# Spreading the routing of the last batch's two halves over the first chunk of expert 0

## The chip, the cores and the metric

The kernel runs on one core of one Trainium2 chip. The metric is the device time of one execution in microseconds (us). The kernel before was timed three times: 938.08, 938.54 and 939.94 us, median 938.54 us.

## The reference

Attention over 32 memory slots per head (4 batches, 8 heads, 576 tokens, head size 64) gives 2304 tokens of width 512. They go through a dense layer pair (512 to 2048, leaky ReLU, back to 512), and then through a mixture of 8 experts with the two best experts per token:

```python
logits = x @ w_gate
noisy_logits = logits + np.log1p(np.exp(x @ w_noise)) * noise
top2 = np.argpartition(-noisy_logits, 2, axis=1)[:, :2]
...
for e in range(E):
    for k in range(2):
        mask = top2[:, k] == e
        h = np.maximum(x[mask] @ w1[e], 0.0)
        out[mask] += top2_w[mask, k, None] * (h @ w2[e])
```

## The kernel before

**Numbers as pairs.** Matrices are held as a high and a low part (`w2h`/`w2l`, `gh`/`gl`, `xh`/`xl`), and a product is three matmuls. ScalarE (ACT) writes the high part by a copy, VectorE (DVE) the low part by a subtraction.

**The dense layers** run in 128 slots `n`. A slot is one batch `b` (0 to 3), one half `u` of its tokens (288 tokens) and one 128-wide piece `f` of the hidden layer. `l1(n)` computes the piece (L587, with L593, L598, L603, L608 behind it), and `l2(n - 2)` multiplies an earlier piece into four output banks (L625); after each fourth piece VectorE adds the banks to the result `big` (L628). Slots 120 to 127 are the last batch (b = 3): four pieces for half 0, four for half 1.

**The routing** of a half is the generator `post(b, u)`: gate logits (`pg` L650, `pl` L656, `lg` L658), the tokens transposed (`px` L665) and written to DRAM as `x2` (L667), the two best experts (L687 to L698), the place of each token in its expert's list by a count (`pr` L702 and L704, then small VectorE operations on `pos`, `blk`, `ri`), matrices of tokens against places (`xr`, L736 to L760), and six matmuls (`pi` L764) that VectorE adds into the lists `acc` (L766). It yields between its parts and runs as a `Job` of ten steps.

**What sets the order.** A job has a start `t0` and a due time `t1` in slots. `tick(t)`, called several times per slot, steps each job that is behind the straight line from `t0` to `t1`:

```python
def behind(self, t):
    return self.did < self.total * (t - self.t0) / max(self.t1 - self.t0, 0.5)
...
tick(len(slots) + 2 + (n + j / 3) * 1.4)   # in expert 0, first chunk, step n
```

A scheduler then places the instructions in each engine's queue. Each queue is worked off in order.

**Expert 0** is done in two chunks: 360 places that hold only tokens of the batches 0 to 2, and 256 places with the rest. For the first chunk the job `early` computes three columns of `get` and `put` (`places`, L770 to L772), gathers three tiles of rows from `x2` (`fetch`, L820, a GpSimd (POOL) indirect DMA into `row`) and transposes them (`turn`: `pxt` L833, `xh` L835, `xl` L836). A chunk has eight pieces of the hidden layer, each 12 matmuls in (`e1`, L858, then `gh` L861 and `gl` L862) and 9 out (`e2`, L876). After the last routing, `handover` computes the other places and fetches the second chunk's two tiles; their `turn` comes when the first chunk ends.

**Expert weights** are loaded by SyncE (SP) in pairs of pieces into two buffers each (`r1` L790, `r2` L792), and split by ScalarE (`w2h` L807) and VectorE (`w2l` L808). A load waits until VectorE has split what was in its buffer. Each call of the generator `weights` splits the two tiles of one piece.

Of the kernel before, what the change touches and what calls it, by code (L numbers as in the profile page):

```python
# [20 lines left out]
def moe_kernel(  # L21
# [18 lines left out]
    B, H, S, D = q.shape  # L40
# [16 lines left out]
    TP = 2  # L57
# [69 lines left out]
    def tick(t):  # L127
        used = 0
        for g in sorted(jobs, key=lambda g: (g.cost >= 0, g.t1)):
            while g in jobs and g.behind(t):  # L130
                if abs(g.cost) + held(g) + used > 2:
                    break
                used += max(g.cost, 0)
                g.step()
# [479 lines left out]
    def l2_db(n, db, eng=None):  # L614
        b, u, f = slots[n]
        first, last = f % 4 == 0, f % 4 == 3
        if first:
            YT[b, u, db] = psum.tile([128, TU], F32, name="py", tag="y", bufs=4)
        ghi, glo, _ = G[n]
        wh, wl = WO[f]  # L620
        py = YT[b, u, db]
        y = Y[:, 2 * b + u]
        s = slice(db * 128, db * 128 + 128)
        for i, (w_, g_) in enumerate(((wh, ghi), (wh, glo), (wl, ghi))):
            nc.tensor.matmul(py, w_[:, s], g_, start=(first and i == 0), stop=(last and i == 2))  # L625
        if last:
            if f > 3:
                nc.vector.tensor_add(y[:, db], y[:, db], py)  # L628
            elif eng is not None:
                eng.tensor_copy(y[:, db], py)  # L630
            else:
                nc.scalar.activation(y[:, db], py, AF.Copy)

    def l2(n):
        b, u, f = slots[n]
        for db in range(NDB):
            l2_db(n, db)
            if db == 1:
                tick(n + 2.5)
        if f == F1 // 128 - 1:  # L640
            Job(post(b, u), 10, n + 2, n + 2 + TP, 1)

    def post(b, u):
        def sm(shape, nm, dt=F32, bufs=2):
            return pp.tile([P] + shape, dt, name=nm, bufs=bufs)
# [55 lines left out]
        for j in range(HJ):  # L701
            nc.tensor.matmul(pr[:P, (j + 1) * E:(HJ + 1) * E], onesb, hit[:, j, None, :].to_broadcast([P, HJ - j, E]),  # L702
                             start=(j == 0), stop=False, skip_group_check=True)
        nc.tensor.matmul(pr[:P, :HJ * E], ups, hit.rearrange("p j e -> p (j e)"), start=False, stop=True,  # L704
                         skip_group_check=True)
        rk = sm([HJ, E], "rk")
        if (b, u) == (B - 1, 0):
            nc.vector.tensor_scalar(cnt[:, 0:1], cnt[:, 0:1], float(CB), None, op0=OP.max)
# [392 lines left out]
    for n in range(8, len(slots) + 2):  # L1101
        if n < len(slots):
            b, u, f = slots[n]
# [42 lines left out]
        if n >= 10:  # L1146
            f2 = slots[n - 2][2]
            while f2 not in WO:
                JW["o", f2 // 4].step()
            l2(n - 2)  # L1150
# [123 lines left out]
```

## Time and profile before

| | |
|---|---|
| median of three executions | 938.54 us (938.08 to 939.94) |
| profiled execution, its own time | 937.07 us |
| its span, first to last instruction | 935.2 us |
| TensorE (PE) busy | 880.1 us, 94% of the span |
| VectorE busy | 539.1 us, 58% |
| ScalarE busy | 356.4 us, 38% |
| mean granted TensorE clock | 0.986 |
| chain that ended last, share on PE | 80%; VectorE 10% |

The chain that ended last is followed back from the last instruction to what released it. A granted clock of 1.00 is 2.4 GHz and 0.50 is 1.2 GHz. Idle time of an engine is put down to the instruction that ended last among those waited for.

### The profile page before, as it was taken

The numbers are of one execution on the slowest core, as the hardware profiler recorded it, in microseconds if no ns is written. First come the engines' busy times: TensorE is split into PE (matmuls) and PEld (weight loads), VectorE is DVE, ScalarE is ACT, GpSimd is POOL, SyncE is SP. The second block draws the span as 40 slices with busy tenths as digits, with TensorE's granted clock in tenths as the row PEclk, the third lists the DMA queues.
The fourth block names the chain that finished last, engine by engine and source line by source line (L and its number), as shares of the span: only waits on it lengthen the run. The fifth ranks groups of instructions, "written<-read, shape, count | busy, mean of one in ns | idle before, by whom it ended". The sixth has DMA issues, their size and how long they took to land.

```text
span 935.2 us, 16252 instructions
## 1 busy us (share of the span) xinstructions
PE 880.1 (94%) x6344; PEld 786.5 (84%) x6344; DVE 539.1 (58%) x1294; ACT 356.4 (38%) x784; POOL 212.6 (23%) x207
## 2 busy tenths in 40 slices
PE   3588999999999999999699999999999999999996
PEld 2377788998999998889588889988988898899885
DVE  5798985456466868788754633544435454452312
ACT  2355665444444544454423433332333323331110
POOL 0051135334300110001003240422305133150302
PEclk9999999999999999999699999999999999999999
DMA  9988712021521201213623652523525434240211
GB/s 221 262 195 179 175 47 90 21 70 46 194 100 46 81 13 49 71 55 90 200 64 110 192 179 91 198 102 129 171 90 181 132 105 167 90 134 1 72 29 57
DMA packets 82615, 105.31 MB, mean 113 GB/s; under 512 B 23988, under 2 KB 58836, under 8 KB 82528
## 3 DMA queue, kind: packets, MB, share of 16 engines
q1 hardware_dynamic: 70528, 71.58, 26.6%
q0 software_dynamic: 9312, 27.88, 9.0%
q10 hardware_dynamic: 2688, 4.72, 1.6%
q8 instruction: 52, 0.85, 0.4%
q14 instruction: 35, 0.29, 0.1%
HBM read 85.88 MB, written 19.53 MB: 113 GB/s over the span
## 4 chain that ended last, share of the span: by engine, by line
PE 80%; DVE 10%; DMA 3%; issue 2%; ACT 2%; SPq 2%; POOL 0%; POOLq 0%; DVEq 0%; ACTq 0%
PE py L876 23%; PE ph L858 23%; PE py L625 18%; PE ph L587 9%; PE pvw L552 2%; PE pxt L833 2%; DMA big<-in_moe_w_out_dram 1%; PE pi L764 1%; DVE mx L360 1%; PE pg L650 1%; DVE mx L330 1%; SPq L194 1%; SPq L173 1%; DMA row<-x,get 1%; DVE wi L214 1%
## 5 line engine op out<-in xcount | busy, mean ns | idle before, releaser
L625 PE MATMUL py<-gh,woh 128*128 128x288 f32 x512 | 155.7, 304 | 3.5 <-ACT gh L603 1.9
L858 PE MATMUL ph<-xh,w2h 128*128 128x256 f32 (+1 forms) x512 | 157.2, 307 | 1.0 <-ACT xh L835 0.6
L858 PE MATMUL ph<-xh,w2l 128*128 128x256 f32 (+1 forms) x512 | 156.7, 306 | 0.0
L858 PE MATMUL ph<-xl,w2h 128*128 128x256 f32 (+1 forms) x512 | 156.1, 305 | 0.0
L808 DVE TENSOR_TENSOR w2l<-r,w2h 128x512 fp32r<-128x512 f32 x128 | 87.6, 687 | 115.5 <-ACT w2h L807 56.6
L625 PE MATMUL py<-gl,woh 128*128 128x288 f32 x512 | 153.3, 299 | 0.4 <-POOL gl L608 0.4
L625 PE MATMUL py<-gh,wol 128*128 128x288 f32 x512 | 152.5, 298 | 0.0
L861 ACT ACTIVATE gh<-ph 128x256 fp32r<-128x256 f32 (+1 forms) x128 | 54.5, 426 | 196.3 <-PE ph L858 186.3
L876 PE MATMUL py<-w2h,gh 128*128 128x512 f32 (+1 forms) x320 | 129.3, 404 | 0.0
L807 ACT ACTIVATE w2h<-r 128x512 fp32r<-128x512 f32 x128 | 79.3, 628 | 128.5 <-PE py L876 96.1
L876 PE MATMUL py<-w2h,gl 128*128 128x512 f32 (+1 forms) x320 | 126.2, 394 | 0.0
L876 PE MATMUL py<-w2l,gh 128*128 128x512 f32 (+1 forms) x320 | 126.1, 394 | 0.0
L862 DVE SCALAR_TENSOR_TENSOR gl<-ph,gh 128x256 fp32r<-128x256 f32 (+1 forms) x128 | 60.6, 473 | 112.3 <-ACT gh L861 103.7
L625 PEld LDWEIGHTS py<-gh,woh 128*128 128x128 f32 x512 | 97.0, 190 | 21.8 <-issue 16.6
L820 POOL DMA_INDIRECT row<-x,get x40 | 44.9, 1122 | 266.7 <-DVE put L771 150.0
L858 PEld LDWEIGHTS ph<-xh,w2h 128*128 128x128 f32 x512 | 97.2, 190 | 7.0 <-ACT xh L835 1.2
L858 PEld LDWEIGHTS ph<-xl,w2h 128*128 128x128 f32 x512 | 97.1, 190 | 3.3 <-DVE xl L836 0.2
L625 PEld LDWEIGHTS py<-gl,woh 128*128 128x128 f32 x512 | 96.9, 189 | 2.5 <-issue 1.4
L625 PEld LDWEIGHTS py<-gh,wol 128*128 128x128 f32 x512 | 97.1, 190 | 1.3 <-issue 1.3
L858 PEld LDWEIGHTS ph<-xh,w2l 128*128 128x128 f32 x512 | 97.0, 189 | 0.0
L598 DVE TENSOR_TENSOR sm<-ph,sm 128x288 f32<-128x288 f32 x128 | 57.7, 451 | 62.4 <-ACT sm L593 61.9
L608 POOL TENSOR_TENSOR gl<-sm,gh 128x288 fp32r<-128x288 f32 x64 | 60.1, 942 | 114.2 <-ACT gh L603 98.2
(163 smaller groups left out, 1520.2 us busy)
## 6 DMA issues: line engine op xcount, KB each, us to landing
r<-in_moe_w_dram SPq DMA_DIRECT2D x64, 512.0 KB, 3.8
raw<-in_moe_w_in_dram SPq DMA_DIRECT2D x16, 512.0 KB, 4.0
raw<-in_moe_w_out_dram SPq DMA_DIRECT2D x14, 512.0 KB, 4.2
out_dram<-zr SPq DMA_DIRECT2D x18, 256.0 KB, 3.8
x<-xr ACTq DMA_DIRECT2D x24, 192.0 KB, 2.2
q<-in_q_dram SPq DMA_DIRECT2D x21, 192.0 KB, 5.0
phi<-in_phi_dram SPq DMA_DIRECT2D x8, 288.0 KB, 3.3
kv<-in_k_dram SPq DMA_DIRECT2D x6, 384.0 KB, 6.6
```

The source lines that it names most:

```text
L552: nc.tensor.matmul(VW[b, c][g][hp * M:(hp + 1) * M, :], VT[b][g * 64:(g + 1) * 64, 1, hp * M:(hp + 1) * M], WI[c, hp][g * 64:(g + 1) * 64, ...
L587: nc.tensor.matmul(ph, w_[:, o:o + 128], a_[:, g], start=(t == 0), stop=(t == 5))
L598: nc.vector.tensor_tensor(sm, ph, sm, op=OP.max)
L608: (eng or (nc.gpsimd if n < NPOOL else nc.vector)).tensor_sub(lo, sm, hi.bitcast(F32))
L625: nc.tensor.matmul(py, w_[:, s], g_, start=(first and i == 0), stop=(last and i == 2))
L807: nc.scalar.activation(h_, src, AF.Copy)
L808: nc.vector.tensor_sub(l_, src, h_.bitcast(F32))
L820: nc.gpsimd.indirect_dma_start(out=xg[:sz], out_offset=None, in_=x2[:(B - 1) * S] if (e, c) == (0, 0) else x2, in_offset=bass.IndirectOffs ...
L858: nc.tensor.matmul(ph[:, :n], w_[:, s], x_[:, db], start=(t == 0), stop=(t == 3 * NDB - 1))
L861: nc.scalar.activation(hi, ph[:, :n], AF.Relu)
L862: nc.vector.scalar_tensor_tensor(lo, ph[:, :n], 0.0, hi.bitcast(F32), op0=OP.max, op1=OP.subtract)
L876: nc.tensor.matmul(PY[c, t][:sz], h_[:, o:o + sz], w_, start=(f == 0 and i == 0), stop=(f == NF2 - 1 and i == 2))
```

## The change

The two halves of batch 3 get a later start and a later due time than two slots each:

```diff
         if f == F1 // 128 - 1:
-            Job(post(b, u), 10, n + 2, n + 2 + TP, 1)
+            t0, t1 = {(B - 1, 0): (n + 4, n + 8), (B - 1, 1): (n + 4, n + 7)}.get((b, u), (n + 2, n + 2 + TP))
+            Job(post(b, u), 10, t0, t1, 1)
+
+    ranked = []
...
+        ranked.append((b, u))
+        assert ranked == sorted(ranked)
```

Half 0 (created at n = 123) moves from the slots 125 to 127 to 127 to 131; half 1 (n = 127) from 129 to 131 to 131 to 134. Times above 130 lie in the first chunk of expert 0, at 1.4 per piece. The assertion runs when the program is built: the halves must be counted in order. Lines below the change stand 3 lines lower in the new file, from L711 on 5 lines lower (L764 is now L769, L833 is L838, L858 is L863, L876 is L881).

TensorE's queue at the end of the dense layers, before: the six matmuls of half 0's lists (L764) stand ahead of the transposes of expert 0's rows and of its first matmul.

```order
L625 MATMUL py<-gh,wol 128x288
L764 MATMUL pi<-xr 128x80 x6
L833 MATMUL pxt<-ident,row 128x128 x8
L833 MATMUL pxt<-ident,row 128x104 x4
L858 MATMUL ph_6055<-xh_5954,w2h 128x360
```

All of the dense layers' matmuls are ahead of L764 here, and all of expert 0 behind it.

The same place now: the transposes stand between the last dense matmuls, the routing's transposes of half 0 (`px`) beside them, and expert 0 follows without L764.

```order
L838 MATMUL pxt<-ident,row 128x128 x4
L668 MATMUL px<-ident,big 96x128 x4
L625 MATMUL py<-gl,woh 128x288
L625 MATMUL py<-gh,wol 128x288
L625 MATMUL py<-gh,woh 128x288
L625 MATMUL py<-gl,woh 128x288
L625 MATMUL py<-gh,wol 128x288
L838 MATMUL pxt<-ident,row 128x104 x4
L668 MATMUL px<-ident,big 96x128 x4
L863 MATMUL ph_6013<-xh_5833,w2h 128x360
L863 MATMUL ph_6080<-xh_5833,w2h 128x360
L668 MATMUL px<-ident,big 96x128 x4
```

L764 went out of this place, the row transposes went up among the dense matmuls, and `px` came down from before them.

Half 0's six matmuls now stand in TensorE's queue behind 48 matmuls L863 and 21 matmuls L881 of expert 0, and half 1's first ones (`pg`) right behind them:

```order
L881 MATMUL py_6152<-w2h,gl 128x512
L769 MATMUL pi<-xr 128x80 x6
L653 MATMUL pg<-big,wgn 32x288 x4
L881 MATMUL py_6156<-w2h,gh 128x512
L881 MATMUL py_6156<-w2l,gh 128x512
L881 MATMUL py_6156<-w2h,gl 128x512
L659 MATMUL pl<-sel,gt 96x16 x3
L668 MATMUL px<-ident,big 96x128 x8
```

Both halves' work moved into expert 0's first chunk; half 1's began three pieces earlier before.

VectorE's queue behind the places of the first chunk, before: half 0's routing starts at once (`lg`), with the weight splits behind and between.

```order
L772 SCALAR_TENSOR_TENSOR put<-acc,put 128x3
L598 TENSOR_TENSOR sm<-ph,sm 128x288
L658 COPY lg<-pl 96x48
L608 TENSOR_TENSOR gl<-sm,gh 128x288 x2
L671 TENSOR_SCALAR uu<-ez 96x24
L808 TENSOR_TENSOR w2l<-r_5387,w2h 128x512
```

Here the routing leads and the split of `r_5387` comes sixth.

Now: five splits and the first low part of expert 0's rows (`xl`) come ahead of it.

```order
L777 SCALAR_TENSOR_TENSOR put<-acc,put 128x3
L598 TENSOR_TENSOR sm<-ph,sm 128x288
L813 TENSOR_TENSOR w2l<-r_5387,w2h 128x512
L608 TENSOR_TENSOR gl<-sm,gh 128x288 x2
L813 TENSOR_TENSOR w2l<-r_5389,w2h 128x512
L813 TENSOR_TENSOR w2l<-r_5387,w2h 128x512
L813 TENSOR_TENSOR w2l<-r_5928,w2h 128x512
L813 TENSOR_TENSOR w2l<-r_5389,w2h 128x512
L841 TENSOR_TENSOR xl_5834<-pxt,xh_5833 128x4x128
L661 COPY lg<-pl 96x48
```

The splits moved up and the routing down; from `lg` to the last of `xr` VectorE now has eleven splits (nine before), two `xl` and three `gl` (L867) between the routing's own operations, and one pair of L608 fewer.

## Rows read from the trace of the kernel before

**Rows 1.** Engines by stage: window, then length, PE, PEld, DVE, ACT, POOL busy, PEclk, DMA, GB/s
```profile
448.71:455.62 6.91, 0.01 (x1) 0.03 (x1) 6.91 (x23) 1.82 (x4) 0.00 (x0) 0.67 0.54 162
455.62:468.10 12.48, 11.31 (x48) 9.35 (x49) 6.88 (x12) 6.06 (x13) 0.00 (x0) 0.50 0.70 235
468.10:499.75 31.65, 31.65 (x180) 27.96 (x180) 14.38 (x69) 5.89 (x14) 1.93 (x2) 1.00 0.14 41
499.75:927.40 427.65, 426.74 (x2486) 381.88 (x2484) 185.55 (x329) 127.97 (x260) 117.83 (x109) 1.00 0.37 120
```

**Rows 2.** Timeline of PE: start, duration, instruction, idle before it and releaser
```profile
448.42 0.29 PE L625 MATMUL py<-gh,wol 128*128 128x288 f32 x1
...
455.62 2.82 PE L764 MATMUL pi<-xr 96*128 96x80 f32 x12 [6.91 <-DVE xr L760]
...
460.71 0.95 PE L833 MATMUL pxt<-ident,row 104*128 104x104 f32 x4 [0.56 <-DVE xl L836]
462.27 0.67 PE L858 MATMUL ph<-xh,w2h 128*128 128x360 f32 x1 [0.61 <-ACT xh L835]
...
499.75 1.03 PE L833 MATMUL pxt<-ident,row 128*128 128x128 f32 x8
```

**Rows 3.** Timeline of DVE: first and last instruction of half 0's chain
```profile
441.94 0.20 DVE L658 COPY lg<-pl 96x48 f32<-96x48 f32 x1 [1.45 <-PE pl L656]
...
455.08 0.40 DVE L760 TENSOR_TENSOR xr<-xr,chosen 96x240 f32<-96x240 f32 x1
```

**Rows 4.** Groups by line on DVE, 441.9 to 455.48: busy us, mean ns
```profile
L808 DVE TENSOR_TENSOR w2l<-r,w2h 128x512 fp32r<-128x512 f32 x9 | 6.1, 681 | 0.0
L628 DVE TENSOR_TENSOR big<-big,py 128x288 f32<-128x288 f32 x4 | 1.8, 446 | 0.0
```

**Rows 5.** Waits from 438.85 to 499.75: total us, times, longest
```profile
ACT w2h L807 <- DMA r<-in_moe_w_dram: 7.5, 5, 4.4
```

**Rows 6.** Timeline of SP: the load that ended ACT's longest wait
```profile
450.07 0.37 SPq L790 DMA_DIRECT2D r<-in_moe_w_dram  x1
```

**Rows 7.** Timeline of POOL: gathers for the first and the second chunk
```profile
439.90 1.04 POOL L820 DMA_INDIRECT row<-x,get  x1 [110.06 <-DVE put L771]
...
442.53 1.90 POOL L820 DMA_INDIRECT row<-x,get  x1 [0.30 <-issue]
484.41 0.98 POOL L820 DMA_INDIRECT row<-x,get  x1 [39.98 <-DVE put L771]
```

**Rows 8.** DMA busy tenths, 440 to 448 in slices of 0.2 us
```profile
DMA  0000000099358608878759896976575577977200
```

**Rows 9.** DMA busy tenths, 484 to 490 in slices of 0.15 us
```profile
DMA  0000000000000199538852973438764200000000
```

**Rows 10.** Engines by stage, columns as in rows 1: around two other waits
```profile
229.60:231.55 1.95, 0.02 (x2) 0.03 (x1) 1.95 (x5) 0.47 (x2) 0.80 (x1) 1.00 0.07 29
...
232.60:236.00 3.40, 3.40 (x16) 3.40 (x16) 2.19 (x5) 0.85 (x2) 1.32 (x1) 0.50 0.24 49
...
547.30:547.80 0.50, 0.06 (x2) 0.04 (x1) 0.41 (x1) 0.43 (x1) 0.16 (x1) 1.00 0.19 74
547.80:552.00 4.20, 4.20 (x24) 3.87 (x25) 3.18 (x6) 3.07 (x7) 2.12 (x2) 1.00 0.49 179
```

**Rows 11.** Chain that ended last: start, us, what (x12 of pi are six matmuls)
```profile
433.94 1.60 PE py L625 x12
...
437.56 1.35 PE pi L764 x12
...
475.21 0.10 PE pr L702 x3
...
482.27 1.36 PE pi L764 x12
483.64 2.01 PE ph L858 x12
485.65 2.08 PE py L876 x9
```

## Prediction, made before the changed kernel ran

> **What bounds the kernel now.** TensorE is busy for 94% of the span, so I read first where it is not, stage by stage, and at which clock. From 499.75 us to 927.40 it is busy for 426.74 of 427.65 us at clock 1.00 [rows 1]: nothing there can be won by moving other engines' work. The hole lies at the change from the dense layers to expert 0. The last dense matmul starts at 448.42 and the next instruction, half 0's `pi` (L764), at 455.62, after 6.91 us of idle time that `xr` (L760) on VectorE ended [rows 2]. Two shorter waits follow, 0.56 and 0.61 us, for the low and the high part of the gathered rows [rows 2]. And the clock: in the idle stretch the mean falls to 0.67, and from 455.62 to 468.10 TensorE works 11.31 us at 0.50 before 1.00 comes back [rows 1].
>
> So the place costs three things: 6.91 us idle; 0.56 + 0.61 = 1.17 us idle; and 11.31 us at half clock, of which full clock would need 5.66. Together 13.7 us.
>
> Why `xr` was late is read from VectorE: half 0's chain runs from `lg` at 441.94 to L760, which ends at 455.48, 13.5 us [rows 3]. In that time VectorE never waits for long; it also does nine weight splits for 6.1 us and the dense layers' four last additions for 1.8 us [rows 4]. Nothing in expert 0's first chunk needs `pi` of half 0: the chunk takes only tokens of the batches 0 to 2. The wait is one of order in TensorE's queue.
>
> **The change, part by part.**
>
> *Removed.* L764 of half 0 no longer stands ahead of expert 0. The 6.91 us go, and with them what made the clock fall. Gain at most 13.7 us, at least 6.9 if the clock falls all the same and stays as long.
>
> *Moved, at no cost.* TensorE executes the same instructions; their number does not change. Both halves' gate, transposes, count and `pi` now lie between matmuls of expert 0, as half 1's did before, where stretch 468.10 to 499.75 shows no idle time [rows 1]. The three writes of `x2` of each half move along; they are read only by the second chunk's gathers. The loads that ScalarE waits for in the trace, 7.5 us in five waits [rows 5], the longest ended by a load that SP could issue only at 450.07 [rows 6], come behind expert 0's four pairs: they are for expert 1. They were late since VectorE freed the buffers late. In the new order the five splits that free them stand ahead of the routing, so I take these waits as gone from TensorE's path.
>
> *Added: the row transposes go up between the last dense matmuls.* They wait for the gathers, and what stands behind them in TensorE's queue waits too. The order is unchanged up to 438.9 us, the end of batch 2's last `pi` [rows 11]. From there 28 dense matmuls lead to the first transpose; twelve take 1.60 us [rows 11], so TensorE gets there at 438.9 + 3.7 = 442.6. The first gather is issued at 439.90 [rows 7], its data end at about 442.8, where the fifteenth slice is 0 [rows 8]; with some tenths for the signal I take 443.1, a wait of 0.5 us. The second tile has time. The third gather's data end at about 447.5 [rows 8], and TensorE gets there by the same addition (17 more dense matmuls, `pg`, `pl`, two transposed tiles and one `px`) at 447.6.
>
> Behind it I walked the three queues with durations of the rows. Short waits: 0.25 us at the third `pxt`, whose bank ScalarE must empty first; 0.3 at the first matmul of expert 0 for `xh`; 0.2 at the last `px` for `xl`; 0.6 at `pr` for VectorE's `hit`; 0.35 at half 1's third `px`. With the first one 2.2 us. None of them stands in the trace; the nearest rows are the 0.56 and 0.61 us that the same copies cost now [rows 2]. Bounds: 0, if every copy comes a little earlier, and 4.4, each of them doubled. I take 2.2, as they are sums of shown durations.
>
> *Added: half 0's `pi` has a new deadline.* The walk puts the first L863 at 448.9. From there 48 of them (2.0 us for twelve, 485.65 - 483.64 [rows 11]), 21 L881 (2.08 for nine [rows 11]), `px` and `pr` with their waits (1.3) bring TensorE to L769 at 463.1. VectorE starts `lg` at 445.7; to the 13.5 us of before come two more splits and two `xl` at about 0.68, three L867 at about 0.5, less two L608, and the wait at `pr`: 16.9 + 0.6, so it ends at about 463.2. It is a tie. Bounds 0 and 2 us; I take 0, as the mean of one split includes overlap with the next.
>
> *Added: the second chunk's gathers come later within the first chunk.* Before, half 1's `pi` ended at 483.64 [rows 11] and its rows were transposed at 499.75 [rows 2], 16 us later. Now, behind half 1's `pi`, TensorE has only 17 L881 and 12 L863: 17 x 0.231 + 2.0 = 5.9 us. The gathers need, after `pi`, 0.77 us to the first issue (484.41 less 483.64) and 4.4 us until the second's data end at about 488.8 [rows 7, 9, 11]: 5.2 us, and the second tile is wanted 0.4 us after the first. It fits by about 1 us. Half 1's chain from `pr` to `pi` has 7.2 us of matmuls to hide in; before, it had 482.27 - 475.21 = 7.1 [rows 11] and TensorE did not wait.
>
> **The sum.** 13.7 - 2.2 = 11.5 us gained. The profiled execution took 937.07 us and would take 925.6. It lies 1.47 us below the median of the runs, 938.54; I carry the gain over: 938.54 - 11.5 = 927.0 us.
>
> **Two rules weighed.** After an idle time of 1.95 us the clock fell to 0.50 for 3.40 us; after one of 0.50 us it stayed at 1.00 [rows 10]. My waits are at most 0.6 us each. The Trainium skill, "TensorE: Matmul & The Clock Gate", section "A second HAM failure mode: psum-queue depth-cycling", says that many very short idle times between groups of matmuls can make the clock swing too. By it the six waits could cost a fall although none is long; the trace has no such cluster, and that is the first rival below.
>
> The third gather's issue took 1.90 us, others 0.98 and 1.04 [rows 7]. The Trainium skill, "SBUF — State Buffer", section "SBUF: two separate sides", says that GpSimd cannot write a gather's descriptors while VectorE holds the port pair that they share. VectorE now does five splits in a row in that stretch; by this rule the third gather could be later still, by about the 0.9 us that it lost here, and the sum would be 10.6.
>
> **The rivals.**
>
> 1. *The clock falls all the same, or the waits double.* For it: the short waits lie within 11 us, and the 1.95 us that sufficed elsewhere is less than their sum. Against it: rows 10's second pair. One fall as in rows 10 costs half of 3.40, 1.7 us; two 3.4. Doubled waits cost 2.2 more. Gain 6 to 9.5 us: 929 to 932.5, middle 930.7.
>
> 2. *The new tie decides, and the end is slower.* Half 1's `pi` waits on VectorE's chain, the gathers start that much later, and TensorE idles at the second chunk's `pxt` (L838). Each us of delay past the 1 us of room is a us of idle time there, and past some 2 us the clock falls as well, so that a wait like the old one, 6.91 us, would cost 13.7 again. For it: the room shrinks from 11 us to 1. Against: half 1's chain has as many matmuls in front as before. It turns slower from a wait of about 6 us on; at 8 us, with 6 at half clock's price, 938.5 - 11.5 + 14 = 941.
>
> 3. *The wait only changes its name.* Expert 0's first matmul needs the gathered rows' parts; if ScalarE had to wait for expert 1's loads ahead of `xh`, as it does before (a split stands between the `xh` in its queue), TensorE would wait some 5 us more, and the clock would fall as now. Against: ahead of `xh` there are now only splits whose data have landed. It leaves 0 to 5 us of gain: 936.
>
> **Chances.** Forecast, 925 to 929: 0.68. Rival 1: 0.20. Rival 3: 0.07, 0.03 of it within 0.2% of the time before. Rival 2: 0.05. A change of under 0.2% (1.9 us) can hardly be told from none here. Faster 0.92, same 0.03, slower 0.05. The range reaches from 924.5 (no new wait costs anything: 938.54 - 13.7 = 924.8, less a little) to 932.0, into rival 1.
>
> **What would show it.** Right: in the profile after, no idle time of PE above 1 us between 438 and 490; clock 1.00 throughout; L838 of the first chunk from 443, the first L863 near 449; `pi` of half 0 near 463 with little wait; the second chunk's first transpose near 488 instead of 499.75; ScalarE's waits for loads gone or off the path. Wrong: a clock of 0.50 there, or a wait over 1 us at L838 for a gather, at L769 for `xr`, or at L863 for `xh`; each names the step that failed.

## The result, and the profile after

| | before | with the change |
|---|---|---|
| median of the runs | 938.31 us (937.87 to 939.94, four) | 926.04 us (924.43 to 926.80, four) |
| ratio | | 0.9871, 95% interval 0.9857 to 0.9885 |
| profiled execution, its span | 937.07 us, 935.2 us | 926.80 us, 924.9 us |

The change takes 12.3 us off; 927.0 us had been predicted (11.5 us off), with a range of 924.5 to 932.0.

The two profiled executions cannot be laid over each other at equal times. The one after starts the `pi` of batch 2's last half at 439.52 us, the one before at 437.39. Two further profiles of the changed kernel lie at 435.49 and 440.43, so this offset belongs to the execution; early on, between 40 and 50 us, the clock granted was 0.50 after and 0.91 before. I therefore measure one **stretch** in every trace: from the first matmul of that `pi` to the first transpose of the second chunk's rows (L838, before L833). Its two ends are the same matmuls in every version. Before, it is 499.75 [rows 2] - 437.39 = 62.36 us, by this row of the kernel before:

```profile
437.39 1.51 PE L764 MATMUL pi<-xr 96*128 96x80 f32 x12
```

Where times of after are compared with times of before, 2.13 us (439.52 - 437.39) are taken off.

The timeline of TensorE after, which answers to rows 2 (start, duration, instruction, idle before it and what ended that):

```profile
439.52 1.51 PE L769 MATMUL pi<-xr 96*128 96x80 f32 x12
...
445.56 0.63 PE L838 MATMUL pxt<-ident,row 128*128 128x128 f32 x4 [0.78 <-DMA row<-x,get]
446.12 0.69 PE L653 MATMUL pg<-big,wgn 128*32 128x288 f32 x8
446.74 0.40 PE L625 MATMUL py<-gl,woh 128*128 128x288 f32 x1
...
450.96 0.55 PE L838 MATMUL pxt<-ident,row 104*128 104x104 f32 x4 [0.29 <-DMA row<-x,get]
...
452.11 0.59 PE L863 MATMUL ph<-xh,w2h 128*128 128x360 f32 x2 [0.17 <-ACT xh L840]
...
466.00 1.46 PE L769 MATMUL pi<-xr 96*128 96x80 f32 x12
...
482.06 1.48 PE L769 MATMUL pi<-xr 96*128 96x80 f32 x12
...
489.33 1.03 PE L838 MATMUL pxt<-ident,row 128*128 128x128 f32 x8
```

The stretch is now 489.33 - 439.52 = 49.81 us, 12.55 less. The reader should see three idle times in it, 0.78, 0.29 and 0.17 us, and that neither `pi` of batch 3 has one. On the clock of before the first transpose starts at 443.4 (443 in the list of what would show it), the first L863 at 450.0 (near 449), the second chunk's transpose at 487.2 (near 488). The engines by stage, columns as in rows 1:

```profile
445.00:452.00 7.00, 6.10 (x51) 5.03 (x51) 5.11 (x14) 4.10 (x11) 1.07 (x1) 1.00 0.86 228
452.00:466.00 14.00, 13.85 (x78) 12.32 (x79) 13.40 (x55) 8.42 (x18) 0.00 (x0) 1.00 0.76 238
466.00:489.33 23.33, 23.33 (x145) 20.12 (x144) 13.22 (x67) 4.51 (x11) 1.92 (x2) 1.00 0.21 64
489.33:917.00 427.67, 426.49 (x2486) 381.84 (x2484) 186.08 (x329) 128.06 (x260) 117.62 (x109) 1.00 0.37 121
```

Ahead of PEclk's 1.00 there stood 0.67 and 0.50 before [rows 1]. Behind the stretch nothing changed: 427.65 us then and 427.67 us now contain 426.7 and 426.5 us of work. VectorE's last operation of half 0's chain, and the third gather on POOL, from their timelines:

```profile
465.20 0.40 DVE L765 TENSOR_TENSOR xr<-xr,chosen 96x240 f32<-96x240 f32 x1
```

```profile
444.72 1.34 POOL L825 DMA_INDIRECT row<-x,get  x1 [0.30 <-issue]
```

The chain ends at 465.60, TensorE comes to `pi` at 466.00. The third gather's issue takes 1.34 us where it took 1.90 [rows 7].

### The profile page after: what moved, and what is told of

The parts are those of the page before. It is cut to its first block, busy times and chain, and to the rows that moved or that the text cites. A ratio compares the mean times of both kernels' runs of the same rounds, so it can differ in the third digit from the quotient of the medians.

```text
span 924.9 us, 16252 instructions
## 1 busy us (share of the span) xinstructions
PE 875.7 (95%) x6344; PEld 784.3 (85%) x6344; DVE 538.7 (58%) x1294; ACT 356.1 (39%) x784; POOL 211.2 (23%) x207
## 4 chain that ended last, share of the span: by engine, by line
PE 82%; DVE 9%; DMA 4%; ACT 2%; issue 2%; POOL 0%; SPq 0%; POOLq 0%; ACTq 0%; DVEq 0%
PE py L881 24%; PE ph L863 24%; PE py L625 18%; PE ph L587 9%; DMA q<-in_q_dram 3%; PE pxt L838 2%; PE pvw L552 2%; PE pi L769 1%; DVE mx L330 1%; DVE mx L360 1%; DVE wi L209 1%; PE pg L653 1%; DMA row<-x,get 1%; DVE wi L214 1%; PE pq L367 1%
## 5 line engine op out<-in xcount | busy, mean ns | idle before, releaser
L863 PE MATMUL ph<-xh,w2l 128*128 128x256 f32 (+1 forms) x512 | 155.9, 305 | 0.0
L863 PE MATMUL ph<-xh,w2h 128*128 128x256 f32 (+1 forms) x512 | 155.7, 305 | 0.2 <-ACT xh L840 0.2
L863 PE MATMUL ph<-xl,w2h 128*128 128x256 f32 (+1 forms) x512 | 155.3, 303 | 0.0
L881 PE MATMUL py<-w2h,gh 128*128 128x512 f32 (+1 forms) x320 | 129.4, 404 | 0.0
L881 PE MATMUL py<-w2h,gl 128*128 128x512 f32 (+1 forms) x320 | 126.3, 395 | 0.0
L881 PE MATMUL py<-w2l,gh 128*128 128x512 f32 (+1 forms) x320 | 126.2, 394 | 0.0
L867 DVE SCALAR_TENSOR_TENSOR gl<-ph,gh 128x256 fp32r<-128x256 f32 (+1 forms) x128 | 60.6, 473 | 100.7 <-ACT gh L866 97.2
L863 PEld LDWEIGHTS ph<-xh,w2h 128*128 128x128 f32 x512 | 96.5, 189 | 5.0 <-ACT xh L840 0.7
L863 PEld LDWEIGHTS ph<-xl,w2h 128*128 128x128 f32 x512 | 96.5, 188 | 3.3 <-DVE xl L841 0.2
L863 PEld LDWEIGHTS ph<-xh,w2l 128*128 128x128 f32 x512 | 96.4, 188 | 0.0
L593 ACT ACTIVATE sm<-ph 128x288 f32<-128x288 f32 x128 | 52.6, 411 | 88.2 <-PE ph L587 82.6
```

The costliest lines, as they stand in the source:

```text
L593: nc.scalar.activation(sm, G[n], AF.Copy, scale=0.01)
L863: nc.tensor.matmul(ph[:, :n], w_[:, s], x_[:, db], start=(t == 0), stop=(t == 3 * NDB - 1))
L867: nc.vector.scalar_tensor_tensor(lo, ph[:, :n], 0.0, hi.bitcast(F32), op0=OP.max, op1=OP.subtract)
L881: nc.tensor.matmul(PY[c, t][:sz], h_[:, o:o + sz], w_, start=(f == 0 and i == 0), stop=(f == NF2 - 1 and i == 2))
```

## The experiments

Each ratio is to the kernel before, timed beside the version on the same chip.

**Which half matters.** Each half alone gets the later times; the diff shows the line of both versions.

```diff
-            t0, t1 = {(B - 1, 0): (n + 4, n + 8), (B - 1, 1): (n + 4, n + 7)}.get((b, u), (n + 2, n + 2 + TP))
+            t0, t1 = {(B - 1, 0): (n + 4, n + 8)}.get((b, u), (n + 2, n + 2 + TP))      # half 0 alone
+            t0, t1 = {(B - 1, 1): (n + 4, n + 7)}.get((b, u), (n + 2, n + 2 + TP))      # half 1 alone
```

> Only half 0 gets the later times; half 1 keeps its two slots (129 to 131). Theory (the gain is half 0's `pi` no longer standing ahead of expert 0, with the idle 6.91 us and the clock that falls after it): nearly the whole gain, 926 to 928 us, clock 1.00 through the turn, no wait over 1 us. Rival (the second half must move too, because the two chains share VectorE and half 0's `pi` was a tie already): half 1's operations lie between those of half 0, `pi` of half 0 waits 1 to 3 us on VectorE, 928 to 931 us.

> Only half 1 gets the later times; half 0 is as before. Theory: the wait of some 7 us at half 0's `pi` and the half clock behind it stay, and half 1's later start gives nothing back: 937.5 to 939.5 us. Rival (what counts is VectorE's queue, which half 1's move clears for the splits): part of the wait goes, 930 to 935 us. If the second chunk's gathers are late because of the move: over 939.5 us, with idle time at the second chunk's first transpose.

Half 0 alone: 925.47 us, ratio 0.9855 (0.9822 to 0.9888), the whole gain (926 to 928 us had been expected). Half 1 alone: 938.67 us, 0.9998 (0.9984 to 1.0013), none of it. TensorE's timeline with half 0 alone, and with half 1 alone:

```profile
437.65 1.51 PE L769 MATMUL pi<-xr 96*128 96x80 f32 x12
...
464.68 1.54 PE L769 MATMUL pi<-xr 96*128 96x80 f32 x12
...
487.41 1.03 PE L838 MATMUL pxt<-ident,row 128*128 128x128 f32 x8
```

```profile
438.94 1.51 PE L769 MATMUL pi<-xr 96*128 96x80 f32 x12
...
457.17 2.82 PE L769 MATMUL pi<-xr 96*128 96x80 f32 x12 [6.91 <-DVE xr L765]
...
501.09 1.03 PE L838 MATMUL pxt<-ident,row 128*128 128x128 f32 x8
```

Stretches of 49.76 and 62.15 us. In the second the old wait stands with the same 6.91 us, and `pi` takes the 2.82 us of the half clock. With half 0 alone both chains lie mixed on VectorE, and `pi` still does not wait: it stands behind 42 L863 and 18 L881 in place of 48 and 21, with half 1's first matmuls among them, and VectorE is done 0.14 us before it. The rival, that the second half must move too, falls.

**The clock by itself.** In the kernel before, TensorE gets work to do while it waits; nobody reads the result.

```diff
         pi = ps_m("pi")
+        if (b, u) == (B - 1, 0):
+            for _ in range(26):
+                nc.tensor.matmul(pi[:, 128:254], ident[:P], ch[:, 0, None, :].to_broadcast([P, 21, 2 * HJ]),
+                                 start=True, stop=True, skip_group_check=True)
```

> The kernel before, with 26 matmuls of 126 columns whose result nobody reads put into the bank of half 0's `pi`; they fill the idle time there (26 x 0.21 = 5.5 of 6.9 us). The wait of `pi` for VectorE stays as long as it was. Theory (the clock falls because TensorE idles, and that costs 5.66 us of its own): clock 1.00 from 448 to 468, `pi` still near 455.6, and the time falls by 5 to 6 us to 932.5 to 933.5 us. Rival (the half clock comes from something else there, or the work behind `pi` waits for others anyway): 937 to 939 us.

931.23 us, ratio 0.9924 (0.9886 to 0.9963), a little more than the 5 to 6 us expected. The timeline of TensorE, and the two windows:

```profile
438.01 1.51 PE L768 MATMUL pi<-xr 96*128 96x80 f32 x12
...
448.89 6.03 PE L765 MATMUL pi<-chosen,ident 96*128 96x126 f32 x52
454.75 0.60 PE L837 MATMUL pxt<-ident,row 128*128 128x128 f32 x4
...
455.93 1.56 PE L768 MATMUL pi<-xr 96*128 96x80 f32 x12 [0.30 <-DVE xr L760]
...
459.03 0.59 PE L862 MATMUL ph<-xh,w2h 128*128 128x360 f32 x2 [0.63 <-ACT xh L839]
...
493.81 1.03 PE L837 MATMUL pxt<-ident,row 128*128 128x128 f32 x8
```

```profile
448.89:455.93 7.04, 6.74 (x61) 6.50 (x59) 7.00 (x24) 2.29 (x5) 0.00 (x0) 1.00 0.65 212
455.93:469.00 13.07, 12.44 (x86) 10.72 (x87) 11.32 (x39) 8.55 (x20) 0.00 (x0) 1.00 0.65 206
```

`pi` comes as late as before, 17.92 us behind batch 2's (18.23 before), and yet the stretch is 55.80 us, 6.56 shorter. Idle time and filler are 0.30 + 0.63 + 5.86 = 6.79 us where 6.91 + 1.17 = 8.08 stood, which is 1.29 of it. The other 5.3 us are the clock, which now stays at 1.00. My term was 5.66, so it holds to 0.4 us, and it is a price of its own: the half clock was the result of the idle time, not of the work behind it.

**Only `pi` moved.** Half 0 keeps its old times for nine steps; the last one comes later.

```diff
-            t0, t1 = {(B - 1, 0): (n + 4, n + 8), (B - 1, 1): (n + 4, n + 7)}.get((b, u), (n + 2, n + 2 + TP))
-            Job(post(b, u), 10, t0, t1, 1)
+            t0, t1 = {(B - 1, 1): (n + 4, n + 7)}.get((b, u), (n + 2, n + 2 + TP))
+            if (b, u) == (B - 1, 0):
+                Job(post(b, u), 25, t0, t0 + 5, 1)
+            else:
+                Job(post(b, u), 10, t0, t1, 1)
...
+        for _ in range(15 if (b, u) == (B - 1, 0) else 0):
+            yield 0
         yield 1
         pi = ps_m("pi")
```

> Half 1 as in the change. Half 0 keeps its old times for its first nine steps and only its last step, the six matmuls `pi`, is handed over later, in the first piece of expert 0. VectorE has half 0's routing ahead of the splits again, as before the change. Theory (only the place of `pi` in TensorE's queue counts): 926 to 928.5 us, with a wait of about 1 us where expert 0's second piece needs its low part, which VectorE splits after the routing. Rival (the gain needs VectorE's new order, splits and low parts ahead of the routing): expert 0 waits 4 us or more for low parts, the clock falls again, 931 to 936 us.

924.97 us, ratio 0.984 (0.980 to 0.988), under the 926 to 928.5 us expected. Its timeline:

```profile
439.18 1.52 PE L774 MATMUL pi<-xr 96*128 96x80 f32 x12
...
449.47 0.55 PE L843 MATMUL pxt<-ident,row 104*128 104x104 f32 x4 [0.28 <-DMA row<-x,get]
...
456.62 1.46 PE L774 MATMUL pi<-xr 96*128 96x80 f32 x12
...
487.89 1.03 PE L843 MATMUL pxt<-ident,row 128*128 128x128 f32 x8
```

Half 0's `pi` runs 17.44 us behind batch 2's, no later than in the kernel before (18.23), and without a wait; only that TensorE has done the end of the dense layers and 27 matmuls of expert 0 in the meantime. VectorE has the routing ahead of the splits as before, and the 1 us that I expected for a late low part does not appear. The rival, that the gain needs VectorE's new order, falls. The stretch is 48.71 us, 1.1 below the change.

**What sets the order.** Half 0's `pi` takes its PSUM bank from another ring of buffers; the jobs keep their old times.

```diff
-        pi = ps_m("pi")
+        pi = ps_m("pi") if (b, u) != (B - 1, 0) else psum.tile([128, 512], F32, name="pi", tag="y", bufs=4)
```

> The kernel before with both halves' old times; only half 0's `pi` takes its PSUM bank from the ring of four (`py`) and not from the ring of two in which the row transposes `pxt` follow it. In TensorE's queue the transposes and 24 matmuls of expert 0 then stand ahead of `pi`. Theory (the wait is one of order, and the order comes from the ring of two banks, not from the times of the job): 924.5 to 927.5 us, clock 1.00, no wait over 1 us between 438 and 490. Rival (the later times themselves are needed, since VectorE has the routing ahead of the low parts and splits): expert 0 waits 3 us or more for `xl`, `w2l` or `xr`, 930 to 937 us.

925.59 us, ratio 0.9879 (0.9859 to 0.9899): one line without any new time gives the gain. In the kernel before, `pi`, the row transposes `pxt` and the routing's other small results (`pg`, `pl`, `px`, `pr`) take turns in two banks, in the order of the code; the second `pxt` needs the bank that `pi` holds, so it cannot stand ahead of `pi`. In the filled version above the first `pxt` does stand ahead of `pi` (454.75), the second behind it. With `pi` in the other ring the transposes and 23 matmuls of expert 0 go ahead. TensorE's timeline:

```profile
436.92 1.51 PE L764 MATMUL pi<-xr 96*128 96x80 f32 x12
...
456.56 1.46 PE L764 MATMUL pi<-xr 96*128 96x80 f32 x12
...
486.91 1.03 PE L833 MATMUL pxt<-ident,row 128*128 128x128 f32 x8
```

TensorE shows no idle time in the stretch, and half 0's `xr` is done 2.6 us before `pi`; yet the stretch is 49.99 us, 1.3 longer than in the version with only `pi` moved; the last section says where that lies.

**The room of the second chunk's gathers.** The change, with half 1's `pi` handed over later (k = 22 or 26 empty steps ahead of it).

```diff
-            Job(post(b, u), 10, t0, t1, 1)
+            if (b, u) == (B - 1, 1):
+                Job(post(b, u), 10 + k, t0, t0 + (t1 - t0) * (10 + k) / 10, 1)
+            else:
+                Job(post(b, u), 10, t0, t1, 1)
...
+        for _ in range(k if (b, u) == (B - 1, 1) else 0):
+            yield 0
         yield 1
         pi = ps_m("pi")
```

> The same with half 1's `pi` 8 L881 and 12 L863 (3.85 us) later than in the change: 15 L881, 3.47 us, lie between it and the second chunk's first transpose. Theory: waits of 0.6 us for the first tile and 0.4 for the second, clock 1.00: 926.5 to 928 us. Rival (more room): no wait, 925.5 to 926.5 us.

> The change, with half 1's last step handed over later, so that in TensorE's queue half 1's `pi` stands 17 L881 and 12 L863 (5.9 us) later than in the change: 9 L881 lie between it and the second chunk's first transpose, 2.08 us, where there were 17 L881 and 12 L863. Theory (the gathers need 4.1 us from the end of `pi` to the first tile's data and 5.4 to the second's): TensorE waits 2.0 us for the first tile and 0.8 for the second, the clock falls behind the first wait as it did after 1.95 us in the kernel before, 1.7 us more: 928.5 to 931 us. Rival (the gathers have much more room than the trace suggests, or do not end the wait): 925.5 to 927 us.

> The change as it is, beside the others on the same chip. Theory (it keeps 1.24 us of short waits that the version with only `pi` moved does not have): 925.5 to 926.8 us, and the stretch from batch 2's last `pi` to the second chunk's first transpose 49.8 us, 1.1 more than in that version.

k = 22: 926.45 us, 0.9882 (0.9861 to 0.9903). k = 26: 930.53 us, 0.9922 (0.9900 to 0.9944). The change beside them: 924.60 us, 0.9865 (0.9843 to 0.9886), under the 925.5 to 926.8 us expected, stretch 485.14 - 435.49 = 49.65 us. TensorE's waits with k = 22, and with k = 26 together with the windows behind:

```profile
485.99 1.46 PE L774 MATMUL pi<-xr 96*128 96x80 f32 x12
...
491.76 0.63 PE L843 MATMUL pxt<-ident,row 128*128 128x128 f32 x4 [0.79 <-DMA row<-x,get]
...
493.33 0.63 PE L843 MATMUL pxt<-ident,row 128*128 128x128 f32 x4 [0.48 <-DMA row<-x,get]
...
494.65 0.50 PE L868 MATMUL ph<-xh,w2h 128*128 128x256 f32 x2 [0.46 <-ACT xh L845]
...
495.63 0.39 PE L868 MATMUL ph<-xl,w2h 128*128 128x256 f32 x1 [0.48 <-DVE xl L846]
```

```profile
488.37 1.46 PE L774 MATMUL pi<-xr 96*128 96x80 f32 x12
...
494.10 1.01 PE L843 MATMUL pxt<-ident,row 128*128 128x128 f32 x4 [2.12 <-DMA row<-x,get]
495.67 1.09 PE L843 MATMUL pxt<-ident,row 128*128 128x128 f32 x4 [0.56 <-DMA row<-x,get]
497.45 0.80 PE L868 MATMUL ph<-xh,w2h 128*128 128x256 f32 x2 [0.69 <-ACT xh L845]
```

```profile
492.00:494.10 2.10, 0.00 (x0) 0.03 (x1) 0.07 (x1) 0.00 (x0) 1.79 (x2) 1.00 0.61 156
494.10:500.96 6.86, 5.61 (x23) 4.62 (x24) 2.29 (x4) 1.23 (x3) 4.12 (x5) 0.51 0.51 171
```

From the end of `pi` to the first transpose, where the data end the wait, pass 491.76 - 487.45 = 4.31 and 494.10 - 489.83 = 4.27 us; to the second tile's transpose 5.88 and 5.84. In the change the two come 489.33 - 483.54 = 5.79 and 6.2 us behind `pi`. So its room is 1.5 us for the first tile and 0.3 for the second. With k = 26 the waits are 3.37 us together, and 5.61 us of work at half clock cost another 2.8 (1.7 expected): 6.2 us, against 5.9 measured. The rival with much more room falls.

**The best version beside the change.** Both once more, on the same chip.

> The version with only half 0's `pi` moved, once more, on the same chip as the change. By the traces its stretch from batch 2's last `pi` to the second chunk's first transpose is 1.1 us shorter than that of the change (48.71 against 49.81 us), since the first gather has landed when TensorE comes to it. If nothing later gives that back: 923.5 to 925.5 us, 1.1 us under the change. If it is given back: the same as the change.

> The change as it is, as the partner of the version with only half 0's `pi` moved: 924.5 to 926.5 us, a short wait of 0.8 us for the first gather as in the two traces of it.

924.57 us, 0.9849 (0.9834 to 0.9864), and 926.49 us, 0.9864 (0.9846 to 0.9883); the stretches are 48.90 and 49.64 us. The traces put the version with only `pi` moved 0.7 to 1.1 us ahead each time. The medians say 1.9 us here; in the runs above, on different chips, they were 924.97 against 926.04 and 924.60 us. The intervals overlap, so by the times alone the two are not told apart.

## Why the prediction was right

**The 13.7 us removed.** Confirmed in both parts. The wait was one of order: with half 0's `pi` out of the way it is gone, with everything else it stays (half 1 alone). The half clock was its consequence, 5.3 us by the filled version against my 5.66. What I had not said is why `pi` stood there: the ring of two banks.

**The six short waits, 2.2 us.** On TensorE's rows the stretch has three idle times: the first gather 0.78 us (I had 0.5), `xh` 0.17 (0.3) and the third gather 0.29, for which I had nothing; together 1.24. The other waits did come, but on the rows of the weight loads (PEld), which go ahead of the matmuls. The last `px`, `pr` and half 1's third `px` waited there in the change:

```profile
452.74 0.39 PEld L668 LDWEIGHTS px<-ident,big 128*96 128x96 f32 x4 [0.33 <-DVE xl L841]
456.40 0.21 PEld L705 LDWEIGHTS <-onesb 96*96 96x96 bf16 x3 [0.20 <-DVE hit L701]
470.57 0.39 PEld L668 LDWEIGHTS px<-ident,big 128*96 128x96 f32 x4 [0.31 <-ACT xr L669]
```

The third `pxt` waited 0.30 us for ScalarE in the profile of the changed kernel that starts at 440.43, where the third gather is not waited for:

```profile
451.66 0.38 PEld L838 LDWEIGHTS pxt<-ident,row 104*128 104x128 f32 x4 [0.30 <-ACT xr L669]
```

The record of a matmul lasts longer than the distance to the next one's start (0.33 against 0.16 us for L863), so a wait shorter than the difference leaves no idle time on TensorE's rows, and a longer one reads too short there. Counted by how much longer the distances between starts are than the same ones without a wait (0.63 us from the two L863 to the last `px` where 0.41 is usual, and so on; an estimate), the three rows of the change above cost 0.22, 0.05 and 0.12 us, the three idle times are 0.94, 0.41 and 0.46 instead of 0.78, 0.17 and 0.29, and all six come to about 2.2 us. My sum was right, its parts were not (`pr` 0.05 for 0.6, the first gather 0.94 for 0.5): that is luck.

**The gain, 12.3 us for 11.5.** The 0.8 us more come from what I had put at nothing or read too short. "Moved, at no cost" was not quite so: the matmuls `pg` of the two halves stand in three lots before, six and two records of half 0 and eight of half 1 at 462.86, and in two lots now, and by the last section a lot fewer saves 0.6 us.

```profile
438.84 0.69 PE L650 MATMUL pg<-big,wgn 128*32 128x288 f32 x6
440.04 0.67 PE L650 MATMUL pg<-big,wgn 128*32 128x288 f32 x2
```

And the idle times before (6.91, 0.56 and 0.61 us) read too short in the same way, by a few tenths. That the bare idle times give 13.7 - 1.24 = 12.5 us, where the stretch shows 12.55 and the medians 12.27, is partly luck, as these terms cancel in it.

**`pi` of half 0, a tie.** VectorE is done at 465.60, TensorE comes at 466.00; on the clock of before that is 463.47 and 463.87, where I had 463.2 and 463.1. It stayed a tie: VectorE is ahead by 0.4 us in all three profiles of the change, and with half 0 alone by 0.14 us (464.54 against 464.68), although `pi` starts there 27.0 us behind batch 2's in place of 26.5. That it fell on the good side is partly luck; a version without the tie is the one with the other bank, 2.6 us.

**The second chunk's gathers.** "Fits by about 1 us" was between what the two tiles have, 1.5 and 0.3 us. The way from `pi` to the second tile's use takes 5.9 us, not 5.2: I had read the end of the data, and the signal and the transpose's start come behind it. The second rival's mechanism is therefore real and near; moving half 1's `pi` by 3.85 us cost short waits (1.9 us by the medians), by 5.9 us it cost 5.9.

**Rival 1.** The clock stayed at 1.00 with the short waits of the change. With k = 22 four waits of 0.79, 0.48, 0.46 and 0.48 us lie within 4 us, and the mean over 490 to 501 us is still 1.00. The Trainium skill, "TensorE: Matmul & The Clock Gate", section "A second HAM failure mode: psum-queue depth-cycling", tells of a clock that swings from many tiny idle times. No run here shows it for waits this many and this short.

**Rival 3.** Among the waits of the stretch there is none of ScalarE for a load any more; 7.5 us stood there [rows 5]. The third gather's issue became no longer either, 1.34 against 1.90 us [rows 7]; it takes 1.33 to 1.35 us in every version in which half 0's routing begins later, and 1.88 to 1.90 in every one in which it begins at the old time. The rule of the Trainium skill, "SBUF — State Buffer", section "SBUF: two separate sides", by which the sum would have been 0.9 us smaller, is not borne out as a loss here: with the splits beside it the issue is the shorter one. Which operations of VectorE make it 1.90 us was not tried.

## What to carry to other kernels

When an engine with an in-order queue waits for a result that nothing behind it needs, ask first what holds the instruction in that place: here it was a shared ring of two buffers, and a buffer from another ring gave the same 12 us as moving the whole routing. Price an idle time of several us on TensorE with the clock behind it, here 5.3 us for 6.9. Where a gain is the end of a wait, the sum of new waits a few tenths long is the least certain term; give it the widest bounds, and look for them afterwards on the weight loads too.

## What the runs showed that I had not expected

The half clock lasted 3.40 us after an idle time of 1.95 us [rows 10], 6.9 us after 2.12 us and two shorter waits with k = 26, and over 12 us after 6.91 us and two shorter waits [rows 1]. The first two differ by a factor of two behind nearly the same idle time, so I would not work out the one from the other; what part the shorter waits have in it was not tried.

Four matmuls `pg` (32 columns of weights each) cost no more than one, if nothing stands between them. The timeline of the version with the other bank, where the scheduler split them:

```profile
449.74 0.67 PE L650 MATMUL pg<-big,wgn 128*32 128x288 f32 x2
450.35 0.43 PE L858 MATMUL ph<-xh,w2h 128*128 128x360 f32 x1
...
452.50 0.68 PE L650 MATMUL pg<-big,wgn 128*32 128x288 f32 x4
453.11 0.43 PE L858 MATMUL ph<-xl,w2h 128*128 128x360 f32 x1
```

One matmul (two records) holds TensorE for 0.61 us until the next starts, two hold it for 0.61, and four in the change, at 446.12 in the first timeline above, for 0.62. That version has the eight matmuls in five lots, the one with only `pi` moved in three: two lots more, 1.2 us, about the 1.3 us by which its stretch is longer. The Trainium skill, "TensorE: Matmul & The Clock Gate", section "Part 3: Packing small matmuls — row/col tiling", says that small matmuls in different parts of the array run at the same time; these rows agree, and another matmul between them ended it here.
